# A fused lightning-attention and PReLU MoE kernel: unit 9's states moved ahead of unit 10's decayed queries, and unit 11's decayed queries moved directly behind a visit

## The chip, the cores and the metric

The kernel runs on one core of a Trainium2 chip. The metric is device time in microseconds: the median of three runs. A core has five engines that run their own instruction queues in order: TensorE (PE in the profile; PEld is its loading of weights), VectorE (DVE), ScalarE (ACT), GpSimd (POOL) and SyncE (SP, here used to issue DMAs). They meet through semaphores. The matrix engine writes to the accumulation memory PSUM; the other operands lie in the on-chip memory SBUF.

## The reference

The input is q, k and v, each 4 batches x 8 heads x 768 positions x 64, and a decay lam per head. The sequence is worked in blocks of 64, with a state per head that is carried on:

```python
for b in range(nb):
    intra = einsum('bhic,bhjc->bhij', qb, kb) * Dmask
    intra = einsum('bhij,bhjd->bhid', intra, vb)
    inter = einsum('bhid,bhde->bhie', qb * lam_pow, kv_state)
    out[:, :, sl] = intra + inter
    kv_state = lam_block * kv_state + einsum('bhsd,bhse->bhde', kb * rev_pow, vb)
```

The result, as 3072 tokens x 512, goes through a layer of two products with a slope for negative values:

```python
h = x @ w_in                                  # 512 -> 2048
g = maximum(h, 0) + alpha * minimum(h, 0)
return g @ w_out                              # 2048 -> 512
```

## The kernel before, in words

**Tiling.** The kernel joins blocks to pieces of 128 positions. A unit is 256 positions (two such pieces) of one batch and four heads; there are 24 units, 0 to 23, four to a chunk. A chunk c is 512 tokens: two batches and all eight heads. Unit n belongs to chunk n // 4, so units 8 to 11 make chunk 2 and units 12 to 15 chunk 3. Per unit the steps are:

- `cast` (line 267): k, q and v from float32 to float16 (`k16`, `q16`, `v16`), on an engine that the call names: "A" ScalarE, "V" VectorE, "G" GpSimd. `key_decayed` (280) makes `kdec`, the keys times their decay.
- `transposes` (297): with "D", a transposing DMA from SyncE's queue, from the cast pair to `qkT`.
- `decayed` (345): the queries times their decay. `qdT` (line 350) is made on the named engine. For units from 8 on there are two more instructions at line 362 that always run on GpSimd: they make `qdX`, half of the queries moved to the other 64 partitions.
- `settle` (608): the unit's new states `R`, four VectorE instructions (line 617) that read the key-value sums out of a PSUM tile `acc`; then two GpSimd copies (line 627) of states to the other 64 partitions, `RX`. The first copies a state that an earlier chunk left, the second one that this settle has just made.
- `visit(olds, news, ...)` (541): TensorE's part of attention for several units at once. For each old unit: queries times states (`outs`, line 509, which reads `R` with `qdT`, and `RX` with `qdX`), then masked scores times values (line 521). For each new unit: scores (line 595, which reads `qkT`), key-value sums (line 573, which reads `kdec` and `v16`). VectorE masks the scores into `sm` (line 605), and ScalarE copies the old units' outputs to `xT`.

For the layer behind it, `up(c, f, ...)` (741) makes one 128-row slice of h for a chunk with four products (line 748); ScalarE makes `m` from it (758) and VectorE the slope product g (780). `down(c, t, part, ...)` (789) does four of the sixteen products of a 128-token output tile (line 795) in a PSUM bank that the call names.

**What sets the order.** The order is written out by hand from line 835 on: a flat list of calls. Each call's instructions are put into their engines' queues in the order of the list, and each engine works its queue in that order. So moving a call in the list moves its instructions in each queue that it uses, past whatever else stands there, and nothing reorders them afterwards. Two calls that use no common engine do not order each other, except through their data.

**Buffers.** Buffers come from pools with a fixed count: `qkT`, `qdT` and `qdX` have three each, the `sm` of each kind two, `kdec`, `v16` and the cast pair four, raw loads five. A new tile waits until all readers of the tile that had its buffer are done. In PSUM, `acc` is one tile for all visits (so a visit's new sums wait for the settles of the visit before), "h" has two banks, and "s0", "s1", "tk" and "op" have one each. A visit puts the first new unit's scores into s0 and s1 and the second's into tk and op.

**Around the change.** The list between lines 1070 and 1114 has: `transposes(10)`, `decayed(10, "G")`, `up(1, 14)`, `cast(11, "v16", "A")`, the last slope products of chunk 1, `cast(12, "k16", "V")`, the `down` calls of chunk 1's first tile, loads, `transposes(11)`, `cast(12, "q16", "V")`, `settle(9)`, `transposes(12)`, then `visit([8, 9], [10, 11], "AA")` at line 1091. Behind it stand `settle(10)`, `key_decayed(14, "G")`, `settle(11)`, `cast(13, "v16", "G")`, `decayed(12, "V")`, casts of units 14, 12 and 13 among which `decayed(11, "V")` stands at line 1100, `transposes(13)`, eight `down` calls, and `visit([10, 11], [12, 13], "AA")` at line 1114. The visit after that, of units 12 to 15, is at line 1139.

Of the kernel before, what the change touches and what calls it, by code (L numbers as in the profile page):

```python
# [11 lines left out]
def kernel(  # L12
# [119 lines left out]
    def bank_of(bank, name, dtype=fp32):  # L132
        pool = h_ps_pool if bank == "h" else ps
        return pool.tile([128, CH], dtype, tag=bank, name=name)
# [117 lines left out]
    def copy_on(eng, out, in_):  # L252
        if eng == "A":
            nc.scalar.activation(out, in_, AF.Copy)  # L254
        elif eng == "V":
            nc.vector.tensor_copy(out=out, in_=in_)  # L256
        else:
            nc.gpsimd.tensor_copy(out=out, in_=in_)  # L258

    def raw_of(n):  # L260
        c, bi, hh = units[n]
        return {
            x + "16": t[:, ds(4 * hh, 4), :].rearrange("p h (e d) -> p e h d", e=2)
            for x, t in zip("kqv", raws[c, bi])
        }

    def cast(n, name, eng):
        t = T.setdefault(n, {})
        if name == "v16":
            t[name] = half_pool.tile([128, 2, 4, D], fp16, tag=name, name=name)  # L270
            copy_on(eng, t[name], raw_of(n)[name])
            return
        if "qk16" not in t:
            t["qk16"] = half_pool.tile([128, 2, 2, 4, D], fp16, tag="qk16", name="qk16")
        copy_on(eng, t["qk16"][:, int(name == "k16")], raw_of(n)[name])

    def engine(x):
        return nc.gpsimd if x == "G" else nc.vector

    def key_decayed(n, eng="G"):  # L280
        hh = units[n][2]
        kr = raw_of(n)["k16"]
        kdec = half_pool.tile([128, 2, 4, D], fp16, tag="kdec", name="kdec")
        engine(eng).tensor_tensor(  # L284
            out=kdec,
            in0=kr,
            in1=kdecay[:, ds(4 * hh, 4), :].rearrange("p h e -> p e h").unsqueeze(3).to_broadcast([128, 2, 4, D]),
            op=ALU.mult,
        )
        T.setdefault(n, {})["kdec"] = kdec  # L290
# [54 lines left out]
    def decayed(n, eng="G"):  # L345
        c, bi, hh = units[n]
        t = T[n]
        qdT = qkt_pool.tile([128, 2, 2, L], fp16, tag="qdT", name="qdT")
        p = ds(64, 64) if c < 2 else ds(0, L)
        engine(eng).tensor_tensor(  # L350
            out=qdT[:, :, :, p],
            in0=t["qkT"][:, 0, :, :, p],
            in1=qdecay[:, hh, :, :, p],
            op=ALU.mult,
        )
        t["qdT"] = qdT
        if c < 2:
            return
        qdX = qkt_pool.tile([128, 2, 2, 64], fp16, tag="qdX", name="qdX")
        for a in range(2):  # L360
            block, other = ds(a * 64, 64), ds((1 - a) * 64, 64)
            nc.gpsimd.tensor_tensor(  # L362
                out=qdX[block],
                in0=t["qkT"][other, 0, :, :, block],
                in1=qdecay[other, hh, :, :, block],
                op=ALU.mult,
            )
        t["qdX"] = qdX
# [161 lines left out]
    def outs_to_xt(n, ot, eng):  # L530
        c, bi, hh = units[n]
        if bi == 0 and hh == 0:
            XT[c] = xt_pool.tile([128, NHP, 2, 2, L], fp16, tag="xT", name="xT")
        x = XT[c][:, ds(2 * hh, 2), :, bi, :].rearrange("p h e (a j) -> p a (h e) j", a=2)
        for a, o in enumerate(ot) if len(ot) == 2 else ():
            copy_on(eng[a % len(eng)], x[:, a], o)
        if len(ot) == 1:
            copy_on(eng, x, ot[0])
        del T[n]

    def visit(olds, news, engs, banks=("tk", "op")):

        acc = ps.tile([128, 2, 512], fp32, tag="acc", name="acc")
        by_h = lambda x: x.rearrange("p (h i) -> p h i", h=2)
        by_j = lambda x: x.rearrange("p (he j) -> p he j", j=64)
        fresh = True
        for i, n in enumerate(olds):
            if i + 1 < len(olds):
                o = [bank_of("h", "ot")[:, 0:256] for a in range(2)]
                view = [by_j(x) for x in o]  # L550
            else:
                o = [acc[:, a, 0:256] for a in range(2)]
                view = [acc[:, :, 0:256].rearrange("p a (he j) -> p a he j", j=64)]
                fresh = False
            outs(n, [by_h(x) for x in o])
            if i + 1 < len(olds):
                outs_to_xt(n, view, engs[i])
            if i == 0 and news:
                wide_scores(news[0], ("s0", "s1"))
        for i, n in enumerate(news):  # L560
            c, bi, hh = units[n]
            pb = c // 2
            t = T[n]
            kv = [acc[:, a, ds(256 + 128 * i, 128)].rearrange("p (h d) -> p h d", h=2) for a in range(2)]
            KV[n] = kv
            for hp in range(2):
                for e in range(2):
                    for hl in range(2):
                        for a in range(2):
                            if 2 * pb + a + 1 == S // L:  # L570
                                continue
                            p = ds(a * 64, 64)
                            nc.tensor.matmul(  # L573
                                kv[a][ds(hl * 64, 64), hp, :],
                                lhsT=t["kdec"][p, e, 2 * hp + hl, :],
                                rhs=t["v16"][p, e, 2 * hp + hl, :],
                                start=(fresh and i == 0 and hp == 0 and e == 0),
                                stop=(e == 1),
                                skip_group_check=True,
                            )  # L580
        if olds:
            outs_to_xt(olds[-1], view, engs[len(olds) - 1])
        elif news:
            wide_scores(news[0], ("s0", "s1"))
        for n in news[1:]:
            wide_scores(n, banks)
# [21 lines left out]
    def settle(n):  # L608
        c, bi, hh = units[n]
        pb, b = c // 2, 2 * (c % 2) + bi  # L610
        kv = KV.pop(n)
        for a in range(2):
            m = 2 * pb + a
            if m + 1 == S // L:
                continue
            for hp in range(2):
                nc.vector.scalar_tensor_tensor(  # L617
                    out=R[b, hh, m + 1][:, hp],
                    in0=R[b, hh, m][:, hp],
                    scalar=rdecay[:, 2 * hh + hp : 2 * hh + hp + 1],  # L620
                    in1=kv[a][:, hp],
                    op0=ALU.mult,
                    op1=ALU.add,
                )
        for a in range(2):
            p, other = ds(a * 64, 64), ds((1 - a) * 64, 64)
            nc.gpsimd.tensor_copy(out=RX[b, hh][p], in_=R[b, hh, 2 * pb + a][other])  # L627
# [107 lines left out]
    G = {}  # L735
# [5 lines left out]
    def up(c, f, bi=None, bank="h", later=False, groups=range(NHP)):  # L741
        if groups[0] == 0:
            HALF[c, f, bi] = bank_of(bank, "h_ps")
        h_ps = HALF[c, f, bi]
        n = CH if bi is None else W
        for gi in groups:
            x = XT[c][:, gi]
            nc.tensor.matmul(  # L748
                h_ps[:, 0:n] if bi is None else h_ps[:, 0:n].rearrange("p (e j) -> p e j", e=2),
                lhsT=w_in_sb[:, gi, ts(f, 128)],  # L750
                rhs=x.rearrange("p e b j -> p (e b j)") if bi is None else x[:, :, bi, :],
                start=(gi == 0),
                stop=(gi == NHP - 1),
            )
        if groups[-1] < NHP - 1:
            return
        m = m_pool.tile([128, CH], fp32, tag="m", name="m")
        nc.scalar.activation(m[:, 0:n], h_ps[:, 0:n], AF.Relu, scale=-1.0)  # L758
        OPEN[c, f, bi] = (h_ps, m)
        if not later:  # L760
            slope_product(c, f, bi)
# [308 lines left out]
    key_decayed(13, "G")  # L1070
    load(3, 1, "k", None)
    transposes(10, "D", False)
    decayed(10, "G")
    up(1, 14, None, "h")
    cast(11, "v16", "A")
    slope_product(1, 15, None)
    up(1, 12, None, "h")
    cast(12, "k16", "V")
    down(1, 0, 0, 4, "op")
    down(1, 0, 1, 4, "op")  # L1080
# [3 lines left out]
    load(3, 1, "q", None)  # L1084
    load(3, 0, "v", None)
    cast(12, "q16", "V")
    settle(9)
    transposes(12, "D", False)
    down(1, 0, 2, 4, "op")
    down(1, 0, 3, 4, "op", True)  # L1090
    visit([8, 9], [10, 11], "AA")
    settle(10)
    key_decayed(14, "G")
    settle(11)
# [2 lines left out]
    cast(14, "k16", "A")  # L1097
    cast(14, "q16", "A")
    cast(12, "v16", "V")
    decayed(11, "V")  # L1100
    cast(13, "q16", "A")
    cast(13, "k16", "A")
    cast(15, "q16", "A")
# [222 lines left out]
```

## Time and profile before

| what | value |
|---|---|
| median of three runs | 213.53 us (212.53 to 214.5) |
| profiled execution, its own time | 213.82 us |
| its span, first to last instruction | 211.7 us |
| TensorE busy | 204.2 us, 96% of the span |
| VectorE, ScalarE, GpSimd busy | 132.3, 115.8, 100.0 us |
| DMA moved | 33.90 MB, mean 160 GB/s |

The span is one execution as the hardware profiler recorded it; the 2.1 us between span and time lie around it. "Busy" is the sum of an engine's instructions; it says how much room an engine has, and not which wait ended last. In the timeline rows the columns are start in us, length in us, engine, line, operation, what is written and read, count, and in brackets idle time before it and what ended that. Names such as `qdX` are those of the program, with buffer numbers left out.

### The profile page before, as it was taken

The page shows a single profiled execution, that of the slowest core. Times are in us where ns is not written, and L with a number is a line of the kernel's source. Part 1 is how long each engine was busy: PE and PEld are TensorE (multiplying, and loading weights), DVE is VectorE, ACT ScalarE, POOL GpSimd, SP SyncE. Part 2 cuts the span into 40 slices and gives each one's busy share as a digit, 9 for nine tenths or more (in the row PEclk, how much of TensorE's full clock was granted, in tenths as well). Part 3 has the DMA queues.
Part 4 walks back from the last instruction along what each step waited for, and adds up shares of the span by engine and source line. Part 5 has one row for each costly group of instructions (what it writes and reads, how often), then busy time and mean ns, then how long its engine had stood idle before and what let it go on. Part 6 is the DMA issues. An engine that isn't in the chain of part 4 may idle for free.

```text
span 211.7 us, 5336 instructions
## 1 busy us (share of the span) xinstructions
PE 204.2 (96%) x2145; PEld 104.0 (49%) x2145; DVE 132.3 (62%) x257; ACT 115.8 (55%) x230; POOL 100.0 (47%) x158
## 2 busy tenths in 40 slices
PE   8997999999999998999999999999999999999994
PEld 7464445645544454545454454544544444444443
DVE  7885787753289977778979884664764344444000
ACT  4896779634685473647544656565534643444121
POOL 7386068350879948967338369419555000000000
PEclk9999999999999999999999999999999999999999
DMA  5999999998999998596983697822201101110212
GB/s 153 292 279 202 215 238 268 221 232 245 285 229 212 245 229 219 117 242 173 180 220 104 134 309 200 245 60 62 87 4 53 50 0 51 53 50 0 99 50 99
DMA packets 62334, 33.90 MB, mean 160 GB/s; under 512 B 18134, under 2 KB 59366, under 8 KB 62310
## 3 DMA queue, kind: packets, MB, share of 16 engines
q1 hardware_dynamic: 58038, 29.37, 55.0%
q0 software_dynamic: 4224, 4.19, 12.3%
q8 instruction: 16, 0.26, 0.5%
q14 instruction: 8, 0.07, 0.1%
q10 hardware_dynamic: 48, 0.01, 0.0%
HBM read 27.27 MB, written 6.29 MB: 159 GB/s over the span
## 4 chain that ended last, share of the span: by engine, by line
PE 86%; POOL 3%; SPq 3%; DMA 2%; DVE 2%; issue 2%; ACT 1%; DVEq 0%; ACTq 0%; POOLq 0%
PE h_ps L748 38%; PE o_ps L795 31%; PE o_ps L824 7%; SPq L93 3%; DMA vraw<-in_v_dram 2%; PE s L595 2%; POOL qdX L362 2%; PE unread L147 1%; PE tp L312 1%; PE acc L573 1%; PE acc L521 1%; PE ot L509 1%; PE s L415 1%; PE ot L521 1%; DVE sm L453 1%
## 5 line engine op out<-in xcount | busy, mean ns | idle before, releaser
L780 DVE SCALAR_TENSOR_TENSOR g<-m,oma,h_ps 128x512 f16<-128x512 f32 (+1 forms) x98 | 70.5, 733 | 46.8 <-ACT m L758 44.6
L748 PE MATMUL h_ps<-xT,w_in_sb 128*128 128x512 f16 (+1 forms) x392 | 91.8, 375 | 0.9 <-ACT xT L254 0.7
L758 ACT ACTIVATE m<-h_ps 128x512 f32<-128x512 f32 (+1 forms) x98 | 57.4, 588 | 47.3 <-PE h_ps L748 46.3
L795 PE MATMUL o_ps<-w_out_sb,g 128*128 128x512 f16 x320 | 77.8, 379 | 0.0
L748 PEld LDWEIGHTS <-w_in_sb 128*128 128x128 f16 x392 | 37.4, 98 | 44.0 <-issue 0.9
L795 PEld LDWEIGHTS <-g 128*128 128x128 f16 x320 | 30.8, 98 | 36.4 <-DVE g L780 0.2
L808 ACT ACTIVATE o_sb<-o_ps 128x512 f32<-128x512 f32 (+2 forms) x25 | 14.5, 580 | 29.5 <-PE o_ps L795 18.3
L350 POOL TENSOR_TENSOR qdT<-qkT,qdecay 128x512 f16<-128x512 f16 (+1 forms) x20 | 19.8, 991 | 11.4 <-ACT qkT L254 7.0
L362 POOL TENSOR_TENSOR qdX<-qkT,qdecay 64x256 f16<-64x256 f16 x32 | 23.6, 736 | 2.5 <-DMA qkT<-qk 0.3
L605 DVE TENSOR_TENSOR sm<-s,dmask 128x512 f16<-128x512 f32 x32 | 20.0, 683 | 6.3 <-PE s L595 6.1
L284 POOL TENSOR_TENSOR kdec<-kraw,kdecay 128x512 f16<-128x512 f32 x17 | 18.5, 1098 | 2.1 <-DMA kraw<-in_k_dram 1.8
L627 POOL COPY RX<-R 64x128 f16<-64x128 f16 x32 | 9.3, 291 | 17.1 <-DVE R L617 15.6
L258 POOL CAST v<-vraw 128x512 f16<-128x512 f32 x12 | 7.3, 612 | 14.7 <-DMA vraw<-in_v_dram 6.8
L824 PE MATMUL o_ps<-w_out_sb,g 128*128 128x512 f16 (+2 forms) x80 | 14.0, 336 | 0.0
L254 ACT ACTIVATE xT<-acc 128x512 f16<-128x512 f32 x16 | 9.5, 597 | 7.5 <-PE acc L442 2.5
L258 POOL CAST qk<-kraw 128x512 f16<-128x512 f32 x12 | 7.8, 662 | 10.2 <-DMA kraw<-in_k_dram 10.1
L824 PEld LDWEIGHTS <-g 128*128 128x128 f16 x80 | 7.2, 97 | 7.0
L617 DVE SCALAR_TENSOR_TENSOR R<-R,rdecay,acc 128x64 f16<-128x64 f16 x48 | 10.2, 273 | 0.0
L258 POOL CAST qk<-qraw 128x512 f16<-128x512 f32 x10 | 6.1, 613 | 2.8 <-DMA qraw<-in_q_dram 2.8
L147 PE MATMUL unread<-ident 128*128 128x512 f16 x23 | 6.6, 413 | 0.3 <-DVE qkT L256 0.3
L453 DVE TENSOR_TENSOR sm<-s,dmask 128x512 f16<-128x512 f32 x8 | 5.1, 684 | 2.5 <-PE s L415 2.5
L595 PE MATMUL s<-qkT 64*64 64x128 f16 x256 | 6.6, 218 | 0.0
(90 smaller groups left out, 159.5 us busy)
## 6 DMA issues: line engine op xcount, KB each, us to landing
out_dram<-o_sb SPq DMA_DIRECT2D x23, 256.0 KB, 2.4
qraw<-in_q_dram SPq DMA_DIRECT2D x10, 512.0 KB, 7.8
kraw<-in_k_dram SPq DMA_DIRECT2D x10, 512.0 KB, 7.3
vraw<-in_v_dram SPq DMA_DIRECT2D x10, 512.0 KB, 6.1
w_in_sb<-in_moe_w_in_dram POOLq DMA_DIRECT2D x4, 512.0 KB, 9.9
w_out_sb<-in_moe_w_out_dram POOLq DMA_DIRECT2D x4, 512.0 KB, 9.8
kraw<-in_k_dram SPq DMA_DIRECT2D x4, 256.0 KB, 4.5
qraw<-in_q_dram SPq DMA_DIRECT2D x4, 256.0 KB, 5.5
```

Of the source, the lines that this page charges most:

```text
L258: nc.gpsimd.tensor_copy(out=out, in_=in_)
L284: engine(eng).tensor_tensor(out=kdec, in0=kr, in1=kdecay[:, ds(4 * hh, 4), :].rearrange("p h e -> p e h").unsqueeze(3).to_broadcast([128, ...
L350: engine(eng).tensor_tensor(out=qdT[:, :, :, p], in0=t["qkT"][:, 0, :, :, p], in1=qdecay[:, hh, :, :, p], op=ALU.mult,)
L362: nc.gpsimd.tensor_tensor(out=qdX[block], in0=t["qkT"][other, 0, :, :, block], in1=qdecay[other, hh, :, :, block], op=ALU.mult,)
L595: nc.tensor.matmul(s[hl][ds(a * 64, 64), hp, 1 - e, :].rearrange("p (e j) -> p e j", e=2), lhsT=t["qkT"][p, 1, e, hp, ds(a * 64, 64)], rhs ...
L605: nc.vector.tensor_tensor(out=sm, in0=s[hl], in1=mask_of(hl, units[n][2]), op=ALU.mult)
L748: nc.tensor.matmul(h_ps[:, 0:n] if bi is None else h_ps[:, 0:n].rearrange("p (e j) -> p e j", e=2), lhsT=w_in_sb[:, gi, ts(f, 128)], rhs=x ...
L758: nc.scalar.activation(m[:, 0:n], h_ps[:, 0:n], AF.Relu, scale=-1.0)
L780: nc.vector.scalar_tensor_tensor(out=g, in0=mv, scalar=oma[:, f : f + 1], in1=hv, op0=ALU.mult, op1=ALU.add)
L795: nc.tensor.matmul(o_ps, lhsT=lhs(c, f, t), rhs=w_out_sb[:, f, :], start=(f == 0), stop=(f == NF - 1),)
L808: nc.scalar.activation(o_sb[:, 0:n], o_ps[:, 0:n], AF.Copy)
L824: nc.tensor.matmul(o_ps[:, 0:n], lhsT=lhs(c, f, t), rhs=w_out_sb[:, f, ds(x, n)], start=(f == 0), stop=(f == NF - 1),)
```

## The change

Two calls and one more change places; no operation is added or dropped, and no engine is changed. `settle(9)` goes from behind `cast(12, "q16", "V")` to ahead of `cast(12, "k16", "V")`. `decayed(10, "G")` goes from directly behind `transposes(10)` to directly behind the new place of `settle(9)`. `decayed(11, "V")` goes from behind `cast(12, "v16", "V")` to directly behind the visit, so that it now stands ahead of `decayed(12, "V")`.

```diff
     transposes(10, "D", False)
-    decayed(10, "G")
     up(1, 14, None, "h")
     cast(11, "v16", "A")
     slope_product(1, 15, None)
     up(1, 12, None, "h")
+    settle(9)
+    decayed(10, "G")
     cast(12, "k16", "V")
     down(1, 0, 0, 4, "op")
     down(1, 0, 1, 4, "op")
...
     cast(12, "q16", "V")
-    settle(9)
     transposes(12, "D", False)
     down(1, 0, 2, 4, "op")
     down(1, 0, 3, 4, "op", True)
     visit([8, 9], [10, 11], "AA")
+    decayed(11, "V")
     settle(10)
     key_decayed(14, "G")
     settle(11)
...
     cast(12, "v16", "V")
-    decayed(11, "V")
     cast(13, "q16", "A")
```

## The prediction

> **What bounds the kernel now.** I read the page first, for which engine has no room.
>
> ```profile
> span 211.7 us, 5336 instructions
> PE 204.2 (96%) x2145; PEld 104.0 (49%) x2145; DVE 132.3 (62%) x257; ACT 115.8 (55%) x230; POOL 100.0 (47%) x158
> ```
>
> PE is busy for 96% of the span. So only a place where PE stands still, or does something later than it could, can move the end. The chain that ended last says where PE was released by another engine. Near the change it reads (start, length, what; "issue" is time in which nothing in the profile was waited for):
>
> ```profile
> 74.40 0.30 POOL RX L627
> ...
> 74.74 0.30 PE acc L509 x6
> ...
> 82.68 1.00 POOL qdX L362
> ...
> 84.48 0.30 PE acc L509 x6
> ```
>
> and POOL's own timeline in front of the first of these places:
>
> ```profile
> 71.16 1.17 POOL L350 TENSOR_TENSOR qdT<-qkT,qdecay 128x512 f16<-128x512 f16 x1
> 72.40 1.59 POOL L362 TENSOR_TENSOR qdX<-qkT,qdecay 64x256 f16<-64x256 f16 x2
> 74.05 0.99 POOL L627 COPY RX<-R 64x128 f16<-64x128 f16 x3
> ```
>
> Twice the chain leaves PE for POOL. In the visit of units 8 to 11 (line 1091; I call it **visit A**) PE's product for unit 9 waits for that unit's moved states RX, which stand in POOL's queue behind unit 10's decayed queries (qdT, qdX, qdX). In the visit of units 10 to 13 (line 1114, **visit B**) PE waits for unit 11's two qdX. From B on the chain holds nothing but PE until the last product, so a microsecond that PE gains there is a microsecond at the end, unless a new wait appears.
>
> The table by stage sizes it. I cut the span at PE's own starts: the stretch before A, visit A, the products between, visit B, the next stretch, and the next visit (line 1139, **visit C**), which does the same work on the next units.
>
> ```profile
> core 0: us, PE busy (x) PEld busy (x) DVE busy (x) ACT busy (x) POOL busy (x), PEclk, DMA share, GB/s
> 73.66:75.68 2.02, 1.91 (x114) 1.58 (x113) 1.79 (x5) 1.22 (x4) 1.20 (x4) 1.00 1.16 296
> 75.68:82.69 7.01, 7.01 (x39) 3.05 (x34) 5.01 (x14) 3.71 (x7) 4.48 (x8) 1.00 0.80 183
> 82.69:85.41 2.72, 1.94 (x113) 1.58 (x113) 1.75 (x3) 1.25 (x4) 2.57 (x3) 1.00 1.07 287
> 95.11:96.63 1.52, 1.52 (x113) 1.43 (x113) 0.73 (x2) 1.24 (x4) 0.33 (x1) 1.00 1.16 290
> ```
>
> The granted clock is 1.00 in each row. Visit C has no stall: 1.52 us. Visit A takes 2.02, so **0.50 too long**; visit B takes 2.72, so **1.20 too long**. That is all the change can address directly: 1.70 us.
>
> **The change, part one: unit 9's states first.** It adds no instruction and moves no DMA. Four VectorE state products and two POOL copies of settle(9) move ahead of two VectorE casts (k16 and q16 of unit 12), and ahead of POOL's qdT and two qdX of unit 10.
>
> ```profile
> 68.28 4.03 DVE L780 SCALAR_TENSOR_TENSOR g<-m,oma,h_ps 128x512 f16<-128x512 f32 x6
> 72.23 0.42 DVE L256 CAST qk<-kraw 128x512 f16<-128x512 f32 x1
> 72.83 0.63 DVE L256 CAST qk<-qraw 128x512 f16<-128x512 f32 x1 [0.18 <-DMA qraw<-in_q_dram]
> 73.38 0.84 DVE L617 SCALAR_TENSOR_TENSOR R<-R,rdecay,acc 128x64 f16<-128x64 f16 x4
> 74.45 2.62 DVE L605 TENSOR_TENSOR sm<-s,dmask 128x512 f16<-128x512 f32 x4 [0.23 <-PE s L595]
> L617 DVE SCALAR_TENSOR_TENSOR R<-R,rdecay,acc 128x64 f16<-128x64 f16 x48 | 10.2, 273 | 0.0
> ```
>
> VectorE's last slope product ahead of this place lets the next instruction start at 72.23. The states would run from 72.23 to 73.07 instead of 73.38 to 74.22. The four start 0.19 apart ((0.84 − 0.27) / 3), so the first two, which the second RX copy needs, end near 72.7. POOL is free for them from 71.16, where qdT starts now; it copies RX once (0.29 in the rows of part two), stands until 72.7, and copies again until about 73.05. So RX of unit 9 is there 0.6 us before visit A begins at 73.66, and 1.6 us before it is there now (74.70). The 0.50 us in A has no cause left.
>
> What is queued behind that new wait on POOL: unit 10's qdT and qdX, which now run from about 73.1 instead of 71.2. They are first read in visit B, nine microseconds later, and POOL stands idle behind visit A in any case (2.48 us in the row below). On VectorE the casts of unit 12 move back: k16 to 73.0, q16 to 73.4 until about 74.0 if it takes 0.63 again. VectorE has 0.23 us idle before the first sm of unit 10, so that sm keeps its start. Behind q16 hangs unit 12's transpose on SP.
>
> This is where the two sides of the cost lie. POOL's qdT of unit 10 now meets VectorE's casts, and such meetings are visible:
>
> ```profile
> L362 POOL TENSOR_TENSOR qdX<-qkT,qdecay x32: 667/672/1184, 64.1 to 161.1; 64x256 f16<-64x256 f16 x32
> 80.56 0.69 DVE L350 TENSOR_TENSOR qdT<-qkT,qdecay 128x512 f16<-128x512 f16 x1 [1.96 <-DMA qkT<-qk]
> 81.17 0.90 DVE L256 CAST v<-vraw 128x512 f16<-128x512 f32 x1
> 82.00 1.16 DVE L350 TENSOR_TENSOR qdT<-qkT,qdecay 128x512 f16<-128x512 f16 x1
> 84.50 1.17 POOL L350 TENSOR_TENSOR qdT<-qkT,qdecay 128x512 f16<-128x512 f16 x1
> 65.06 0.69 DVE sm L605
> 65.80 4.48 PE L748 MATMUL h_ps<-xT,w_in_sb 128*128 128x512 f16 x20 [0.19 <-DVE sm L605]
> ```
>
> A qdX that takes 672 ns at the median took 1184 beside VectorE's qdT, the next cast on VectorE 0.90, and the second qdT there 1.16 where the first took 0.69. At one end, q16 takes 0.63 as now, the masks keep their start, and A gains 0.50. At the other end, POOL's qdT (1.17 us) starts between the two casts, at about 73.4, and q16 stands until 74.5 and ends at 74.85. Then the first sm of unit 10 ends near 75.5 instead of 75.14, and PE's next product needs it: down(1, 1, 0) writes the bank s0 that this sm reads. The last two rows show the same dependence behind the earlier visit, where PE restarted 0.05 us after an sm ended (65.06 + 0.69 = 65.75, then 65.80). PE would go on at 75.55 instead of 75.68: a gain of 0.13. The nearest row is the q16 cast itself, which already meets a qdX (0.63), but the POOL instruction that it now meets is longer; I take **0.2 us** for part one and keep 0.13 and 0.50 for the range.
>
> The Trainium skill, page "SBUF — State Buffer", section "SBUF: two separate sides", speaks against part one: the port pair that VectorE and GpSimd share is an exclusive lock, held for a whole instruction, and whoever comes second stands still. The rows above agree in kind (1184 against 672). By this rule alone the lower end would hold, and the sum would be 1.33 us; by the q16 row (0.63) it would be 1.70.
>
> **Part two: unit 11's decayed queries directly behind visit A.** One VectorE qdT and two POOL qdX move ahead of two settle calls (eight state products, four RX copies), kdec of unit 14, two v16 casts and unit 12's own qdT and qdX. Now they stand behind unit 12's transpose:
>
> ```profile
> 77.52 0.29 POOL L627 COPY RX<-R 64x128 f16<-64x128 f16 x1 [2.48 <-DVE R L617]
> 77.89 1.05 POOL L284 TENSOR_TENSOR kdec<-kraw,kdecay 128x512 f16<-128x512 f32 x1
> 79.00 0.64 POOL L627 COPY RX<-R 64x128 f16<-64x128 f16 x2
> 79.70 0.61 POOL L258 CAST v<-vraw 128x512 f16<-128x512 f32 x1
> 80.61 3.82 POOL L362 TENSOR_TENSOR qdX<-qkT,qdecay 64x256 f16<-64x256 f16 x4 [0.30 <-DMA qkT<-qk]
> ```
>
> The four qdX are unit 12's and then unit 11's. All four wait at 80.6 for a transpose that only the first two need, and unit 11's end at 84.44. After the change POOL has ended unit 10's work by about 73.1 + 1.17 + 2 × 0.67 + three gaps of 0.08 (77.89 − 77.52 − 0.29) = 75.85 (up to 0.4 later when it meets the casts), so unit 11's qdX run until about 77.3, five microseconds before PE needs them. Unit 11's keys and queries have landed by then, since PE's scores read them inside visit A. VectorE's qdT (0.69 to 1.16) starts when the four masks end, at 74.45 + 2.62 = 77.07, and pushes the states of units 10 and 11 back by as much.
>
> What is late next? POOL goes on with RX of unit 10 behind its states (two of them end at 78.1 to 78.6), then kdec 1.05, RX 0.64, v16 of unit 13 0.61, with gaps of 0.08 done by 80.7 to 81.2, then unit 12's qdX behind its transpose as now. Visit B would start near 82.5. When it needs what is read off visit B now (unit 12's scores) and off visit C (the key-value sums):
>
> ```profile
> 83.05 0.39 PE L595 MATMUL s<-qkT 64*64 64x128 f16 x16
> 96.03 0.42 PE L573 MATMUL acc<-v,kdec 64*64 64x64 f16 x32
> ```
>
> The scores come 0.36 after the start (83.05 − 82.69), the sums 0.92 after it (96.03 − 95.11), so unit 13's values are first needed at 83.4. Unit 13's transpose is issued at 78.35 (rival 1) behind ScalarE casts that stay, and its scores are the last of the visit. So nothing of the list is late, and B falls from 2.72 to C's 1.52: **1.20 us**.
>
> **Sum.** 0.2 + 1.2 = 1.4 us off the profiled execution, 213.82 us (span 211.7, 2.1 around it), which gives 212.4. That execution lies 0.29 above the median of the three runs, 213.53; off the median it is **212.1 us** (211.8 without the collision). The three runs lie 2 us apart, so about 1% is what a measurement of this kernel can tell from no change; my gain is 0.7%.
>
> **The rivals.**
>
> 1. *The wait goes over to unit 12's transpose.* Its q16 is ready up to 1.4 us later (74.85 for 73.46). For it: now the transpose is the first of the two issued from 73.52 on, the second follows at 78.35, and the qdT at 80.56 above waits for the first to land.
>
> ```profile
> 73.52 6.13 SPq L302 DMA_TRANSPOSE qkT<-qk  x2
> 78.35 1.30 SPq L302 DMA_TRANSPOSE qkT<-qk  x1
> ```
>
> Visit B reads it first at 82.9, and v16 of unit 12 stands behind it on VectorE. A landing 1.4 later than 80.5, at 81.9, costs PE about 0.2 through that v16; 1.2 more and part two is eaten: 213.3. Against it: the DMA engines' share is 1.16 in visit A and 0.80 over the 7 us behind it, so the transpose mostly waits for bytes ahead of it, not for its issue. Chance 0.2, for 212.7 to 213.5.
>
> 2. *Slower: collisions stretch POOL's list ahead of visit B.* Eleven POOL instructions (three of unit 10, two of unit 11, four RX, kdec, v16) would stand between 73.1 and what visit B needs last of them. By the rows above one collision costs 0.5 (1184 − 672). The list ends near 80.9, the need is at 83.4: 2.5 us of room. It decides from 2.5 + 1.4 = 3.9 us, eight collisions of eleven; with all of them, 5.5 us, visit B is 3.0 late and the time is 213.53 + 3.0 − 1.4 = 215.1. Against it: only the two casts and qdT of VectorE's work in that stretch have shown it; the states and masks read PSUM and leave RX at 0.29. Chance 0.07.
>
> 3. *More than the two stalls.* The casts do not meet, A gives 0.50, and the POOL work 2 us earlier spares waits further on: 211.3. Against it: PE shows no waits behind B. Chance 0.08.
>
> 4. *The change does not do what it says*, because units 9 and 11 still wait for something else: 213.5. The order of the code is the order of each engine's queue in every row above, so 0.05.
>
> **How the numbers follow.** The forecast has 0.6. The middle of the range is 212.1; the two ends of part one make it 211.8 to 212.2, the spread of a median of runs (half of the 2 us) 211.1 to 213.1, and rivals 1 and 4 carry it to 213.8 above; rival 3 to 210.9 below. More than 1% faster is under 211.4: rival 3, and a fifth of the forecast by the spread, 0.2. More than 1% slower is over 215.7, past rival 2's full price and so only with the spread on top or with a cost that no row shows: 0.08. The rest, 0.72, is within 1%.
>
> **What would show it.** Right, step by step: POOL's two RX copies of unit 9 stand before unit 10's qdT and end near 73; visit A takes 1.5 to 1.9 us; POOL's qdX of unit 11 end before 78; visit B takes about 1.5, and the chain no longer leaves PE for POOL in either. A collision shows as a q16 cast of unit 12 over 0.9 us and an sm that ends after 75.3. Wrong: a PE wait in visit B on unit 12's scores or values, a later visit over 1.6 us, or the stretch between A and B over 7.0.

## The result, and the profile after

The changed kernel takes **211.93 us** (median of nine runs, 211.43 to 212.44), the kernel before 213.53 us (nine runs beside them). The ratio is **0.9927, 95% interval 0.9905 to 0.9949**: 1.6 us or 0.7% faster. The forecast was 212.1 us.

The page of the changed kernel, with the shares of the chain that ended last:

```profile
span 210.3 us, 5339 instructions
PE 202.3 (96%) x2145; PEld 103.1 (49%) x2145; DVE 131.6 (63%) x257; ACT 116.0 (55%) x230; POOL 100.1 (48%) x158
PE 90%; DMA 3%; DVE 2%; issue 1%; SPq 1%; ACT 0%; POOL 0%; DVEq 0%; ACTq 0%
```

PE's share of the span is 96% as before, so the busy shares say nothing of this change. The chain does: POOL has no share left in it (3% before). In order of time it now runs through both visits on PE alone:

```profile
73.84 0.24 PE ot L509 x8
74.08 0.22 PE ot L521 x16
74.30 0.22 PE s L595 x16
74.53 0.11 PE acc L509 x8
74.64 0.22 PE acc L521 x16
74.86 0.25 PE acc L573 x32
75.11 0.23 PE s L595 x16
75.34 7.04 PE o_ps L795 x32
82.38 0.24 PE ot L509 x8
```

The table by stage, cut at the same places as before (visit A, the products between, visit B, and visit C):

```profile
core 0: us, PE busy (x) PEld busy (x) DVE busy (x) ACT busy (x) POOL busy (x), PEclk, DMA share, GB/s
73.77:75.31 1.54, 1.54 (x113) 1.45 (x113) 0.84 (x3) 1.26 (x4) 1.46 (x2) 1.00 1.17 294
75.31:82.31 7.00, 7.00 (x36) 3.03 (x33) 5.09 (x14) 3.68 (x7) 6.34 (x11) 1.00 1.07 189
82.31:83.81 1.50, 1.50 (x113) 1.41 (x113) 0.70 (x2) 1.24 (x4) 1.36 (x3) 1.00 1.13 325
93.52:95.05 1.53, 1.53 (x114) 1.44 (x113) 0.73 (x2) 1.25 (x4) 0.42 (x1) 1.00 1.16 290
```

A fell from 2.02 to 1.54 us and B from 2.72 to 1.50: 0.48 + 1.22 = 1.70 us, and both are now as short as C. PE came to A 0.11 later in this execution (73.77 for 73.66), and 1.59 earlier to C (93.52 for 95.11). From the start of A to the start of C it took 1.70 less. The span fell by 1.4.

POOL's and VectorE's timelines of the changed kernel, from unit 9's copies on:

```profile
72.11 0.29 POOL L627 COPY RX<-R 64x128 f16<-64x128 f16 x1
72.87 0.29 POOL L627 COPY RX<-R 64x128 f16<-64x128 f16 x1 [0.48 <-DVE R L617]
73.24 1.65 POOL L350 TENSOR_TENSOR qdT<-qkT,qdecay 128x512 f16<-128x512 f16 x1
74.97 3.23 POOL L362 TENSOR_TENSOR qdX<-qkT,qdecay 64x256 f16<-64x256 f16 x4
78.26 0.63 POOL L627 COPY RX<-R 64x128 f16<-64x128 f16 x2
78.98 1.05 POOL L284 TENSOR_TENSOR kdec<-kraw,kdecay 128x512 f16<-128x512 f32 x1
80.09 0.99 POOL L627 COPY RX<-R 64x128 f16<-64x128 f16 x2
81.14 0.68 POOL L258 CAST v<-vraw 128x512 f16<-128x512 f32 x1
```

```profile
72.34 0.85 DVE L617 SCALAR_TENSOR_TENSOR R<-R,rdecay,acc 128x64 f16<-128x64 f16 x4
73.11 0.42 DVE L256 CAST qk<-kraw 128x512 f16<-128x512 f32 x1
73.44 0.42 DVE L256 CAST qk<-qraw 128x512 f16<-128x512 f32 x1
74.57 0.69 DVE L605 TENSOR_TENSOR sm<-s,dmask 128x512 f16<-128x512 f32 x1 [0.70 <-PE s L595]
```

Unit 9's second copy ends at 73.16, before visit A starts. POOL's qdT of unit 10 did meet the casts, but it was POOL that stood (1.65 for 1.17) and not q16 (0.42). Unit 11's last qdX ends at 78.20 instead of 84.44.

### The profile page after: what moved, and what is told of

Same layout as the page of the kernel before. It is cut to its first block, busy times and chain, and to the rows that moved or that the text cites. A ratio compares the mean times of both kernels' runs of the same rounds, so it can differ in the third digit from the quotient of the medians.

```text
span 210.3 us, 5339 instructions
## 1 busy us (share of the span) xinstructions
PE 202.3 (96%) x2145; PEld 103.1 (49%) x2145; DVE 131.6 (63%) x257; ACT 116.0 (55%) x230; POOL 100.1 (48%) x158
## 4 chain that ended last, share of the span: by engine, by line
PE 90%; DMA 3%; DVE 2%; issue 1%; SPq 1%; ACT 0%; POOL 0%; DVEq 0%; ACTq 0%
PE h_ps L748 39%; PE o_ps L795 33%; PE o_ps L824 7%; DMA vraw<-in_v_dram 3%; PE s L595 2%; SPq L93 1%; PE unread L147 1%; PE tp L312 1%; PE acc L573 1%; PE ot L509 1%; PE acc L521 1%; PE ot L521 1%; PE s L415 1%; DVE sm L453 1%; PE acc L677 1%
## 5 line engine op out<-in xcount | busy, mean ns | idle before, releaser
L362 POOL TENSOR_TENSOR qdX<-qkT,qdecay 64x256 f16<-64x256 f16 x32 | 22.8, 711 | 2.3
L284 POOL TENSOR_TENSOR kdec<-kraw,kdecay 128x512 f16<-128x512 f32 x17 | 17.7, 1047 | 1.3 <-DMA kraw<-in_k_dram 1.0
L258 POOL CAST qk<-kraw 128x512 f16<-128x512 f32 x12 | 8.5, 718 | 12.0 <-DMA kraw<-in_k_dram 11.9
L254 ACT ACTIVATE v<-vraw 128x512 f16<-128x512 f32 x10 | 6.2, 624 | 0.4 <-DMA vraw<-in_v_dram 0.4
```

Source lines behind the costliest of these rows:

```text
L284: engine(eng).tensor_tensor(out=kdec, in0=kr, in1=kdecay[:, ds(4 * hh, 4), :].rearrange("p h e -> p e h").unsqueeze(3).to_broadcast([128, ...
L362: nc.gpsimd.tensor_tensor(out=qdX[block], in0=t["qkT"][other, 0, :, :, block], in1=qdecay[other, hh, :, :, block], op=ALU.mult,)
```

## The experiments

The theory: PE stood twice for things that POOL did too late, and POOL's order is the cause in both places. The rivals are those of the prediction, and one more that came up with the result: that the stalls are not lengths which can be taken off one by one, but **appointments**, times at which POOL is ready, whenever PE comes. In the table A and B are taken from PE's starts in one profiled execution each; ratios are to the kernel before, run beside them.

| kernel | visit A, us | visit B, us | ratio | 95% interval |
|---|---|---|---|---|
| before | 2.02 | 2.72 | 1 | |
| the change | 1.54 | 1.50 | 0.9927 | 0.9905 to 0.9949 |
| part one alone | 2.00 | 3.49 | 1.0002 | 0.9973 to 1.0032 |
| part two alone | 3.23 | 1.50 | 0.996 | 0.9936 to 0.9985 |
| states early, queries not | 2.50 | 1.50 | 0.9956 | 0.9929 to 0.9984 |
| queries late, states too | 1.54 | 1.50 | 0.9942 | 0.9913 to 0.9971 |
| states in two halves | 1.54 | 1.50 | 0.9911 | 0.9877 to 0.9945 |
| transpose behind the visit | 1.54 | 1.50 | 0.9927 | 0.9899 to 0.9955 |
| banks changed | 1.54 | 1.50 | 0.9916 | 0.9889 to 0.9944 |
| two more POOL products | 1.54 | 2.29 | 0.996 | 0.9933 to 0.9987 |
| part one, no meeting | 1.54 | 3.41 | 1.003 | 0.9997 to 1.0062 |
| part two, no meeting | 1.92 | 1.50 | 0.9947 | 0.9930 to 0.9964 |
| all three | 1.54 | 1.50 | 0.9922 | 0.9893 to 0.9952 |
| the change, same chip | 1.54 | 1.50 | 0.9922 | 0.9887 to 0.9956 |

### Each part alone

Part one alone against before:

```diff
-    decayed(10, "G")
     up(1, 14, None, "h")
...
     up(1, 12, None, "h")
+    settle(9)
+    decayed(10, "G")
     cast(12, "k16", "V")
...
-    settle(9)
```

> Part one alone (unit 9's states and unit 10's decayed queries moved; unit 11's decayed queries left at line 1100). Theory of sums, as the prediction priced it: the two stalls are separate, so visit A falls from 2.02 to about 1.54 us and the time by 0.5 us, ratio 0.998. Rival, the stall of visit B is an appointment and not a length: unit 11's last qdX ends when unit 12's transpose has landed and four qdX have run (84.4 in the profile of before), whenever PE comes. Then A falls to 1.54, B grows by the same 0.5 from 2.72 to about 3.2, and the time does not move: ratio 1.000.

Part two alone:

```diff
     visit([8, 9], [10, 11], "AA")
+    decayed(11, "V")
     settle(10)
...
-    decayed(11, "V")
```

> Part two alone (unit 11's decayed queries directly behind visit A; the rest as before). Both theories: visit A keeps 2.0 us, visit B falls to 1.5, the time falls by 1.2 us, ratio 0.994. If the two parts together are worth 1.56 us and the parts add, this leaves 0.4 for part one; under the rival part one is worth its 0.4 only in company.

Part one alone is worth nothing that these runs can see, 1.0002; the interval also holds the 0.998 of the sums. Its profile does not say it cleanly either, because in that execution the price that the prediction had kept as its lower end was paid. VectorE, POOL and PE of part one alone:

```profile
73.11 0.42 DVE L256 CAST qk<-kraw 128x512 f16<-128x512 f32 x1
73.44 1.39 DVE L256 CAST qk<-qraw 128x512 f16<-128x512 f32 x1
74.76 0.68 DVE L605 TENSOR_TENSOR sm<-s,dmask 128x512 f16<-128x512 f32 x1
```

```profile
73.24 1.31 POOL L350 TENSOR_TENSOR qdT<-qkT,qdecay 128x512 f16<-128x512 f16 x1
```

```profile
75.03 0.42 PE L595 MATMUL s<-qkT 64*64 64x128 f16 x16 [0.20 <-DMA qkT<-qk]
75.49 0.81 PE L795 MATMUL o_ps<-w_out_sb,g 128*128 128x512 f16 x3
```

POOL's qdT ran until 74.55, and q16 ended 0.28 behind it (74.83). The first sm ended at 75.44, and PE went on at 75.49, 0.05 later: the chain of the prediction's lower end, step for step. A was 2.00. There was a second delay in it, which hid behind the first: PE waited for unit 11's transpose before its last scores, which began at 75.03. In the change 0.37 us pass from there to the next product (74.94 to 75.31), so this delay by itself would have held PE until about 75.40; the mask held it until 75.49. In part two alone q16 took 1.29 in the same way, now in front of unit 9's states, and A took 3.23. So both were run again with q16 and unit 12's transpose behind visit A, where they cannot meet POOL's qdT ahead of A:

```diff
-    cast(12, "q16", "V")
...
-    transposes(12, "D", False)
...
     visit([8, 9], [10, 11], "AA")
+    cast(12, "q16", "V")
+    transposes(12, "D", False)
```

> Part one alone once more, with cast q16 of unit 12 and its transpose behind visit A, so that q16 cannot meet POOL's qdT ahead of A (in the first run of part one alone it did: 1.39 us, and visit A stayed at 2.0). Unit 11's decayed queries stay behind unit 12's. Sums: A 1.54, B about 2.7, ratio 0.997. Appointment: A 1.54, but B ends when unit 11's qdX end, near 84.4, so B takes 3.2 or more and the ratio is 1.000.

> Part two alone once more, with q16 of unit 12 and its transpose behind visit A for the same reason (in the first run of part two alone q16 stood 1.29 us in front of unit 9's states). POOL still has unit 10's decayed queries ahead of unit 9's copies, so the copies end near 74.7 at the earliest: A takes 1.9 to 2.5 us depending on when PE comes, B 1.5, ratio 0.994 to 0.995. If the loss of part two alone (0.996 instead of 0.994) was the meeting, this gains it back.

The table by stage of part one without the meeting (A, then B), and POOL's and PE's rows in its B:

```profile
73.30:74.84 1.54, 1.54 (x114) 1.45 (x113) 0.74 (x2) 1.26 (x4) 1.45 (x2) 1.00 1.10 267
81.84:85.25 3.41, 2.11 (x114) 1.68 (x113) 2.35 (x4) 1.26 (x4) 3.18 (x4) 1.00 1.04 285
```

```profile
80.45 3.81 POOL L362 TENSOR_TENSOR qdX<-qkT,qdecay 64x256 f16<-64x256 f16 x4 [0.30 <-DMA qkT<-qk]
```

```profile
84.31 0.21 PE L509 MATMUL acc<-qdX,RX 64*64 64x128 f16 x1 [0.53 <-POOL qdX L362]
```

A is repaired, 1.54, and PE comes to B 0.85 us earlier than before (81.84 for 82.69): 0.48 from A, and 0.36 because it had come to A earlier in this execution (73.30 for 73.66). It ends B only 0.16 earlier (85.25 for 85.41), because the four qdX stand behind unit 12's transpose and end at 84.26 (84.44 before). In the first run of part one alone they began and ended later:

```profile
81.17 3.82 POOL L362 TENSOR_TENSOR qdX<-qkT,qdecay 64x256 f16<-64x256 f16 x4 [0.38 <-DMA qkT<-qk]
```

There they end at 84.99, and B ended at 85.97. So in three executions PE came to B at 81.84, 82.48 and 82.69, and each time it left B 0.97 to 0.99 us behind the end of the last qdX: **the stall at B is an appointment**, and what A gains is given back there. The ratio agrees: 1.003, with an interval that lies above the 0.997 of the sums. Part two without the meeting:

```profile
72.30:74.22 1.92, 1.81 (x114) 1.58 (x113) 1.12 (x2) 1.22 (x4) 1.67 (x5) 1.00 1.16 292
81.23:82.73 1.50, 1.50 (x114) 1.41 (x113) 0.70 (x2) 1.25 (x4) 1.42 (x2) 1.00 1.16 340
```

B is repaired, A is not, and the ratio is 0.9947, 1.1 us. With part two in place, part one then is worth about its stall: from 0.9947 to 0.9927 (the ratio of the change, and also of the change with q16 and the transpose behind A) is 0.43 us, where A falls from 1.92 to 1.54, by 0.38. The intervals of the two overlap, so it is the profile that shows this step. Whether the meeting explains why the first run of part two alone was 0.996 stays open for the same reason.

### Which half of part one

States early on VectorE, but unit 10's queries left in their old place on POOL; and POOL's order as in the change, with the states left behind the casts on VectorE:

```diff
     transposes(10, "D", False)
+    decayed(10, "G")
...
     settle(9)
-    decayed(10, "G")
```

```diff
     up(1, 12, None, "h")
-    settle(9)
-    decayed(10, "G")
     cast(12, "k16", "V")
...
     cast(12, "q16", "V")
+    settle(9)
+    decayed(10, "G")
     transposes(12, "D", False)
```

> As the change, but unit 10's decayed queries stay directly behind their transpose, so on POOL they stand ahead of unit 9's moved copies; VectorE makes unit 9's states early as in the change. If POOL's order is what held visit A: the copies start at 74.05 again, A takes 1.9 us, time 0.4 above the changed kernel, ratio to before 0.994. If VectorE's order is what mattered: A takes 1.54 and the time is that of the change, 0.9927.

> As the change on POOL (copies of unit 9 ahead of unit 10's decayed queries), but the states stay behind the two casts on VectorE, where before has them. If POOL's order alone is the cause: the second copy ends near 74.2, before PE needs it (74.4), A takes 1.55 us and the time is that of the change, 0.9927 of before; POOL's list ahead of visit B ends about 1 us later, at 82.8, still ahead of the 83.2 at which PE needs unit 13's values. If VectorE's half is needed: A takes 1.8 to 2.0 us, ratio 0.995.

POOL and PE with the states early and the queries not:

```profile
71.28 1.16 POOL L350 TENSOR_TENSOR qdT<-qkT,qdecay 128x512 f16<-128x512 f16 x1
72.52 1.49 POOL L362 TENSOR_TENSOR qdX<-qkT,qdecay 64x256 f16<-64x256 f16 x2
74.07 0.72 POOL L627 COPY RX<-R 64x128 f16<-64x128 f16 x2
```

```profile
74.49 0.24 PE L509 MATMUL acc<-qdX,RX 64*64 64x128 f16 x1 [0.42 <-POOL RX L627]
```

The copies stand behind the queries at 74.07 as foretold, although their states are long made, and PE waits; A took 2.50 and not 1.9, since PE came 0.39 earlier than before (73.27) to the same appointment, and PE's next step waited for the second copy. With POOL's order alone A is 1.54 and the ratio 0.9942. The second copy and PE's use of it in that run:

```profile
74.88 0.29 POOL L627 COPY RX<-R 64x128 f16<-64x128 f16 x1 [1.46 <-DVE R L617]
```

```profile
75.70 0.22 PE L509 MATMUL acc<-qdX,RX 64*64 64x128 f16 x2
```

The copy ended at 75.17, 0.5 before PE used it. PE came to A late in this execution, at 75.11, but that is not what repaired A, since POOL was late as well: it was free for unit 10's queries at 73.07. Had they stood first, as before, the copies would have begun 2.89 later (71.16 to 74.05 in the kernel before) and the second would have ended 0.65 behind that: at about 76.6 by this estimate, 0.9 after PE's use. So **POOL's order is the cause**. VectorE's half of part one was not needed in that execution; its interval reaches from below the change's ratio to above it, so what the half is worth in the median stays open.

### The price of a meeting

An order in which, it was thought, POOL's qdT would begin between the two casts. The states and copies of unit 9 are the same instructions, the states now in two halves:

```diff
-    settle(9)
-    decayed(10, "G")
-    cast(12, "k16", "V")
+    settle_half(9, 0)        # two of the four states
+    moved(9)                 # the two POOL copies
+    cast(12, "k16", "V")
+    settle_half(9, 1)
+    decayed(10, "G")
```

> As the change, but on VectorE the order is: first half of unit 9's states, cast k16 of unit 12, second half of the states (which read PSUM), cast q16. POOL's qdT of unit 10 then begins while VectorE is between the two casts. If a meeting makes the second comer wait for the whole of the other's instruction: q16 takes 1.2 to 1.4 us instead of 0.42, the first sm of unit 10 ends near 75.4 or later, PE restarts 0.05 behind it, visit A takes 1.7 to 2.0 us and the time is 0.2 to 0.4 us above the change. If the two only slow each other: q16 takes about 0.6, visit A 1.54, time as the change (0.9927 of before).

POOL and VectorE of that kernel:

```profile
72.55 1.51 POOL L350 TENSOR_TENSOR qdT<-qkT,qdecay 128x512 f16<-128x512 f16 x1
```

```profile
72.62 0.42 DVE L256 CAST qk<-qraw 128x512 f16<-128x512 f32 x1
```

The meeting came, and the other side paid: POOL's qdT has the earlier start, 72.55, and yet q16 took 0.42 and qdT 1.51. The first expectation failed. Of the second, visit A and the time came as said, but q16 was not slowed at all. It is still a wait for a whole instruction: q16 ended at 73.04 and qdT at 74.06, 1.02 later. In the change qdT ended 1.03 after q16 (74.89 and 73.86), and in part one alone 1.02 after k16 (74.55 and 73.53). So it is, at 1.01 to 1.03, in all ten profiled executions in which qdT stood behind a cast. The start in the profile does not tell who loses. Of the five profiled executions with POOL's copies and qdT, and VectorE's states, k16 and q16, in the order of the change (part one alone, the change twice, the banks, the two products), POOL stood in four with qdT at 1.64 to 1.65, and q16 in one. What decides it stays open.

### Rival 1: the transpose

The change with q16 and unit 12's transpose behind visit A (the edit above):

> As the change, but cast q16 of unit 12 and unit 12's transpose go behind visit A, so the transpose is issued about 3.4 us later (77.4 instead of 73.9). Rival 1 of the prediction, taken further: if the transpose's landing follows its issue, it lands past 83 and visit B waits, 2.0 us or more, with unit 12's qdT and v16 behind it. If it mostly waits for bytes ahead of it: it lands by 81, visit B stays at 1.5 us. And q16 can no longer meet POOL's qdT ahead of visit A, so A stays 1.54 in every execution: ratio 0.992 or a little below, at best 0.990.

SyncE's queue and VectorE's qdT of unit 12, first in the change:

```profile
73.93 5.25 SPq L302 DMA_TRANSPOSE qkT<-qk  x2
```

```profile
80.16 0.76 DVE L350 TENSOR_TENSOR qdT<-qkT,qdecay 128x512 f16<-128x512 f16 x1 [0.96 <-DMA qkT<-qk]
```

and then with the transpose behind the visit:

```profile
77.24 1.68 SPq L302 DMA_TRANSPOSE qkT<-qk  x1
```

```profile
80.34 0.69 DVE L350 TENSOR_TENSOR qdT<-qkT,qdecay 128x512 f16<-128x512 f16 x1 [0.93 <-DMA qkT<-qk]
```

Issued at 77.24 instead of 73.93, it is there at 80.3, where the change has it at 80.2. B stays 1.50 and the ratio 0.9927. Rival 1 is out even at more than twice the delay that it was priced for. That says nothing of a much longer delay: here the transpose landed 3.1 us after its issue (6.2 in the change), and 3.1 is the shortest of any transpose in the kernel before.

### Rival 2: POOL's room ahead of visit B

```diff
     decayed(11, "V")
+    idle_product(13)         # kdec of unit 13 once more, into a tile nobody reads
+    idle_product(13)
     settle(10)
```

> As the change, with two more POOL products of 1.05 us into a scratch tile behind unit 11's decayed queries (extra work that nothing reads). It measures the room of POOL's list ahead of visit B, which the prediction put at 2.5 us before collisions and the trace of the change at 1.4 us (v16 of unit 13 ends at 81.82, PE takes it up at 83.2 to 83.4). By the trace: 2.24 us more leave visit B waiting 0.7 to 0.8 us, B takes 2.2 to 2.3 us and the time is 0.8 above the change, ratio 0.996. By the prediction's 2.5 us: B stays 1.5, no loss.

POOL and PE of that kernel (its line numbers are 11 higher from `settle` on; L584 is the key-value sums):

```profile
78.11 2.17 POOL L505 TENSOR_TENSOR scratch_g<-kraw,kdecay 128x512 f16<-128x512 f32 x2
...
83.31 0.61 POOL L258 CAST v<-vraw 128x512 f16<-128x512 f32 x1
```

```profile
83.61 0.68 PE L584 MATMUL acc<-v,kdec 64*64 64x64 f16 x32
```

B takes 2.29, 0.79 longer, for 2.17 + 0.07 = 2.24 us more on POOL. If what lies beyond the room reaches PE in full, the room in the change is **1.45 us**. The trace of the change gives nearly the same without that condition: v16 ended at 81.82 and PE's sums that read it began at 83.23, 1.41 later. So in this run a microsecond on POOL beyond the room was a microsecond on PE, and v16 of unit 13, the end of rival 2's list, is what comes last.

### Further on: a stall that was not part of the change

```diff
-    up(1, 3, None, "s1")
-    up(1, 2, None, "s0")
+    up(1, 3, None, "s0")
+    up(1, 2, None, "s1")
```

> As the change, and the banks of up(1, 3) and up(1, 2) trade places (s0 for the first, s1 for the second). In the changed kernel PE stands 0.53 us at 65.4 until the second sm of unit 8 has read s1; s0 was read 0.6 us earlier. If that stall is on the path: PE is 0.5 us ahead at visit A and to the end, ratio to before 0.990. If the gain is given back: PE reaches the first down of chunk 1 before VectorE's slope products, or visit A before the second moved copy or before unit 11's transpose; then A or the stretch in front of it grows by as much, ratio 0.9927 as the change.

> The change, with unit 12's q16 and transpose behind visit A and with the banks of up(1, 3) and up(1, 2) changed. Each alone was 0.9927 and 0.9916. If both are worth what their traces show (no meeting; 0.13 us of PE's stall at 65 us): 0.1 to 0.3 us below the change, ratio 0.991 to 0.992.

> The changed kernel itself, on the chip and beside the runs of the three above: ratio 0.9927 within its interval; visits A and B at 1.5 us if q16 does not meet POOL's qdT in the profiled execution, A up to 2.0 if it does.

PE in the change, and then with the banks changed:

```profile
64.68 1.04 PE L748 MATMUL h_ps<-xT,w_in_sb 128*128 128x512 f16 x4
65.91 4.48 PE L748 MATMUL h_ps<-xT,w_in_sb 128*128 128x512 f16 x20 [0.19 <-DVE sm L605]
```

```profile
64.95 5.53 PE L748 MATMUL h_ps<-xT,w_in_sb 128*128 128x512 f16 x24
```

A product more takes 0.216 us where nothing stops PE (32 of this size took 7.07 and 20 took 4.48, so 12 took 2.59), and four take 0.86. In the change the fifth begins 1.23 after the first (64.68 to 65.91): PE stood there for 0.37. With the banks changed the row shows no gap any more, but from the start of these 24 products to the start of visit A it is 8.96 us (64.95 to 73.91) where it was 9.09 (64.68 to 73.77): only 0.13 is gained. By this rate the 24 products would take 5.34 and they took 5.53, so half of the stall is still among them; why is not shown. With the banks, and with unit 12's q16 and transpose moved as well, the ratios are 0.9916 and 0.9922 beside 0.9922 for the change itself, all within each other's intervals. No version was found that is measurably faster than the change.

## Why the prediction was right, point by point

- **What bounds the kernel.** Right: two places where PE waited for POOL, 1.70 us together, and 1.70 us is what left visits A and B.
- **Part one, how it works.** Right. The copies end 0.6 us before A, as worked out, the second one behind a wait of 0.48 for the states. The run with POOL's order alone adds that this order did it.
- **Part one, its size.** Mis-sized: 0.2 was taken, 0.48 came. The step is the choice between the two ends by "the POOL instruction that it now meets is longer". The meeting took place, but POOL stood through both casts, which nothing in the prediction's rows could have told: that the upper end came was luck. The lower end is real too (q16 at 1.39 in part one alone, where PE went on 0.05 behind the mask), only rarer in these profiles.
- **The skill's rule**, from "SBUF — State Buffer", section "SBUF: two separate sides" of the Trainium skill, that the shared port pair is held for a whole instruction: the trace of part one alone agrees, q16 at 1.39 until POOL's 1.31 was over. That section of the Trainium skill also lets the one that starts first go through, and by the starts in the profile the change does not agree: qdT started at 73.24, q16 at 73.44, and it was qdT that stood. Whether a start in the profile is the moment at which the ports are taken, no run here shows. The 1.33 us that the rule gave for the sum would have been too little, because which of the two waits came out the other way.
- **Part two.** Right: 1.2 foretold, 1.22 in the trace. Unit 11's last qdX ended at 78.2 and not 77.3, and POOL's list at 81.8 and not 81.2 at the latest, so its sign "before 78" was missed by 0.2. The meetings of POOL's list made it longer by about 1.2 us (qdT 1.65 for 1.17, four qdX at 3.23 where two pairs of 1.40 and a gap make 2.9, RX 0.99 for 0.63, v16 0.68 for 0.61). The room behind it was 1.45 and not 2.5 us, and enough.
- **The sum.** 1.4 foretold, 1.6 by the medians. It added the two stalls, and that held only because both went. The prediction did not see that the stall at B is an appointment, although its own row has the four qdX waiting at 80.6 for a transpose: part one alone gives 1.0002 and, without the meeting, 1.003, and not 0.998.
- **The rivals.** 1 (the transpose) is out, 2 (POOL's list) did not decide, its meetings costing 1.2 of the 3.9 us that it needed, but it names the resource that is next, 3 did not come (no wait further on was spared), 4 is out: visit C starts 1.59 earlier, the last output tile's products 1.64 earlier (193.32 for 194.96 in the chain).

## What to carry to other kernels

Ask of each stall whether it is a length or an appointment: follow the late engine back to what it waited for. If that is a transfer or its own queue and not the waiting engine, a gain further up is lost there, and the last stall of such a chain has to be removed first. On an engine that works in order, put what is read next ahead of what is read later, even where it has to stand and wait for its operand, as long as what stands behind has room; and measure that room by adding work until the next engine waits.

## What the runs showed of the hardware that was not expected

- Where a VectorE cast and POOL's qdT met, the loser waited until the other instruction was over (q16 1.39 for 0.42, qdT up to 1.65 for 1.17), but the loser is not the one with the later start: with starts of 73.11 (k16), 73.24 (POOL's qdT) and 73.44 (q16) in two kernels, qdT stood once through both casts (1.65), and once q16 stood through qdT.
- PE reaches visit A at times that lie 2.8 us apart (72.30 with part two and no meeting, 75.11 with POOL's order alone). The edits are not the reason: the same four products of line 748, which stand ahead of these edits in the list, began at 63.21 and 66.02 in the two executions. Single profiles can thus be compared from visit A on, not by their spans.
- A DMA transpose issued 3.3 us later landed 0.2 us later. That the bytes of the loads ahead of it set its time fits the trace of the change: the DMA engines moved 265 to 308 GB/s in each microsecond from 73 to 78 and 4 in the next one, and it landed only behind that, 6.2 us after its issue. No run separates this from other causes.
